# Streamed operands fetched two at a time in 4 KB rows, and one unit buffer more in the retention stage

## The chip, the core and the metric

The kernel runs on one NeuronCore of a Trainium2 chip. The metric is device time in microseconds (us), the median of several runs; a change is read against the median of the kernel before.

## The reference, cut to what matters

```python
# 1. retention: B, H, S, D = 4, 8, 768, 64 (float32 inputs)
for t in range(S):
    state = gamma * state + einsum('bhd,bhe->bhde', k[:, :, t], v[:, :, t])
    y[:, :, t] = scale * einsum('bhd,bhde->bhe', q[:, :, t], state)
x = y.transpose(0, 2, 1, 3).reshape(3072, 512)
# 2. first feed-forward network, weights float64, 512 -> 2048 -> 512
h = x @ w_in;  g = h / (1 + exp(-1.702 * h));  x = g @ w_out
# 3. second one, own float64 weights, same sizes
h = x @ w_in2;  g = maximum(h, 0) ** 2;  out = g @ w_out2
```

## The kernel before, in words

**Retention.** The 3072 tokens are 24 units of 128 tokens (6 per batch entry). One unit is two tiles of 128 x 1024 floats, 512 KB each, of `qkv`, loaded by `load_unit` (L465) on SyncE's queue (SP); the second tile of every sixth unit is a half. `UNITS = 6` unit buffers are cycled: for unit `u`, `u % UNITS` 0 to 2 lie in the pool `att`, whose three buffers come round every six units, and 3 to 5 (`WIDE = 3`) in the pool `wa`, which has eight. Units are worked in groups: 0 to 3 alone, then pairs, then 22 and 23 alone. Step k of the loop issues, in this order: the scores of group k on TensorE (L493), the output matmuls of group k-1 (`outputs`: L558 the state, L572 within the unit, L587 across units) with ScalarE's copies of the state (L563), `cv_high` (ScalarE, L167), the masks of group k on VectorE (L502), `cv_group` (VectorE: `cv_low` L172 of the weight tile converted last, then `convert` of one more, L143 and L152), the scaling of group k-1 out of PSUM (`scaled`, L609 and L616), `cv_ahead` (loads of float64 weight tiles on GpSimd's queue (POOL), L129, and ScalarE's L137), and the loads of units `u + UNITS` for the units just finished. Each pair's outputs but those of groups 1 and 22 use one PSUM tile `yp`, free again when `scaled` has read it.

**Converted weights.** A float64 weight tile (512 KB, `raw`) is turned into a high and a low float32r part by ScalarE and VectorE. There are 32 tiles for the first network, in the list `order`: 0 is up column 0; 1 and 2 are up column 1 and down row 0; 3 and 4 up column 2 and down row 1; and so on, with up column 8 at place 16. `CONV = 3` of them are converted in the retention stage, from step `CV0 = 12` on, and loads begin at step `RAWU = 9` with at most three ahead of the conversion; after that `up` of the first block runs `cv_step` twice for each of its 16 columns.

**First network, three blocks of 1024 tokens.** The first 1024 tokens and half of the next are done plainly: `up` (L682 to L684), `down` (L712 to L714). The others, and all of the second network, use products of quadrants (seven products in place of eight): `up2` (products 1, 2, 6, 5, 7 of column pair p, with 4 and 3 of the pair p-1 behind 1) and `down2` (28 steps of 12 matmuls). All their matmuls are issued at L923 into banks named X, Y, Z (up) and D (down). The left operands are sums of weight quadrants. `make_first` and `make_second` compute them on VectorE and ScalarE (in `background`, between the matmuls), write them to DRAM tiles `kw` on POOL's queue (L276, L338; plain quadrants on SP's, L291 to L295), and `fetch` (L804) reads them back on SP's queue as tiles `r` of 256 KB, 128 rows of 2 KB each, into `SLOTS = 8` buffers. In `up2` one product reads one tile and frees it, and `fetch` then refills it; in `down2` one step reads two tiles, and frees them.

**Order.** Every engine runs its instructions in the order in which this program issues them. SP's queue holds the unit loads, later the `r` tiles and the loads of kept blocks (L1145); POOL's holds the float64 loads (L129, L264), the makers' writes and the stores of kept results.

Of the kernel before, what the change touches and what calls it, by code (L numbers as in the profile page):

```python
# [10 lines left out]
F32 = mybir.dt.float32  # L11
F32R = mybir.dt.float32r
# [7 lines left out]
P = 128  # L20
# [10 lines left out]
WA = 8  # L31
LOOK = 2
WARM = 9
UNITS = 6
WIDE = 3
XHELD = 4
NL = NT // (2 * TB)
NQ = NF // 2
# [1 line left out]
QS = (11, 12, 21, 22)  # L40
PAD = 96
NSTD = 2
SLOTS = 8
EARLY = 2
BG = 4.7
BGK = (2.6,) * 4 + (1.55,) * 9 + (0.5, 1.4, 0.8)
CV0 = 12
RAWU = 9
CONV = 3
FILL = 6  # L50
RAWS = 5
PL = 4
# [5 lines left out]


A11, A12, A22, S1, S2, S3, S4 = range(7)  # L60
PLACE = (range(7), (0, 1, 2, 4, 5, 3, 6))
B11, B21, B22, T1, T2, T3, T4, B12 = range(8)
PRODUCT = {1: (A11, B11), 2: (A12, B21), 3: (S4, B22), 4: (A22, T4), 5: (S1, T1), 6: (S2, T2), 7: (S3, T3)}

# [2 lines left out]
def tile_retention_then_two_ffns(  # L67
# [73 lines left out]
    def join(out, hb):  # L141

        v.tensor_scalar(out=out, in0=hb, scalar1=3, scalar2=None, op0=ALU.logical_shift_left)  # L143

    def round_up(w, raw):

        def halves(t):
            return t.rearrange("p (c t) -> p c t", t=2)

        half = halves(w.bitcast(U16))[:, :, 0]  # L150
        low = raw.bitcast(U16).rearrange("p c (t u) -> p c t u", u=2)[:, :, 0, 1]
        v.scalar_tensor_tensor(out=half, in0=low, scalar=2.0 ** -13, in1=half, op0=ALU.mult, op1=ALU.add)  # L152

    def cv_a():
# [40 lines left out]

    def cv_ahead(k):

        if k >= RAWU:
            cv_load()
        n = cv["a"]  # L200
        if n < min(cv["load"], cv["b"] + 2) and cv["step"] >= loaded[n] + 2:
            cv_a()
# [15 lines left out]
    def weights(f, s):  # L218
        while (f, s) not in ws:
# [9 lines left out]

    jobs = [(m, i) for m in range(2) for i in range(NJ)]  # L230

    kw = [
        [
            [dr_p.tile([7, P, 2, 256], F32, tag=f"kw{l}{m}{p}", name=f"kw{l}{m}{p}") for p in range(NQ)]
            for m in range(2)
        ]
        for l in range(2)
    ]
    made = set()
    acts = deque()  # L240

# [24 lines left out]
    def make_first():  # L266

        load(0)
        load(1)
        with tc.tile_pool(name="k1", bufs=2, side="right", reuse_waits="tile") as pool:  # L270

            def low(m, p, t, h, done):
                while not done:
                    yield None
                v.tensor_tensor(out=h[:, :, :, 1], in0=t, in1=h[:, :, :, 0], op=ALU.subtract)
                nc.gpsimd.dma_start(  # L276
                    out=kw[0][m][p][S1:S4 + 1].rearrange("i p k c -> p i (k c)"),
                    in_=h.bitcast(F32).rearrange("p i k h c -> p i (k h c)"),
                )
                made.add((0, m, p))  # L280
                yield 1.25

            last = None
            for m in (1, 0):
                for p in range(NQ):
                    w0, w1 = ws[p, m], ws[NQ + p, m]

                    dst = kw[0][m][p].rearrange("i p k c -> p i (k c)")
                    f0, f1 = (w.bitcast(F32).rearrange("p (j k) h c -> p j (k h c)", j=2) for w in (w0, w1))
                    if m == 0:  # L290
                        nc.sync.dma_start(out=dst[:, A11:A12 + 1], in_=f0)  # L291
                        nc.sync.dma_start(out=dst[:, A22], in_=f1[:, 1])
                    else:
                        nc.sync.dma_start(out=dst[:, A11], in_=f0[:, 0])
                        nc.sync.dma_start(out=dst[:, A12:A22 + 1], in_=f1)  # L295
                    w = pool.tile([P, 8, P], F32, tag="w", name=f"wf_{m}_{p}", bufs=1)
                    v.tensor_tensor(out=w[:, 0:4], in0=w0[:, :, 0], in1=w0[:, :, 1], op=ALU.add)
                    yield 0.7
                    v.tensor_tensor(out=w[:, 4:8], in0=w1[:, :, 0], in1=w1[:, :, 1], op=ALU.add)
                    yield 0.7  # L300
                    q0, q1, q2, q3 = (w[:, 2 * k:2 * k + 2] for k in range(4))
                    a11, a12, a21, a22 = (q0, q1, q2, q3) if m == 0 else (q0, q2, q1, q3)
                    t = pool.tile([P, 4, 2, P], F32, tag="t", name=f"wt_{m}_{p}")
                    s1, s2, s3, s4 = (t[:, k] for k in range(4))
                    v.tensor_tensor(out=s1, in0=a21, in1=a22, op=ALU.add)
                    v.tensor_tensor(out=s3, in0=a11, in1=a21, op=ALU.subtract)
                    yield 0.85
                    if last is not None:
                        yield from low(*last)
                    v.tensor_tensor(out=s2, in0=s1, in1=a11, op=ALU.subtract)  # L310
                    v.tensor_tensor(out=s4, in0=a12, in1=s2, op=ALU.subtract)
                    h = pool.tile([P, 4, 2, 2, P], F32R, tag="h", name=f"wh_{m}_{p}")
                    done = later(lambda t=t, h=h: nc.scalar.copy(out=h[:, :, :, 0], in_=t))
                    last = m, p, t, h, done
                    yield 0.85
            yield from low(*last)

    def make_second():

        with (  # L320
# [12 lines left out]
            def low(n, w, t, done):  # L333
                while not done:
                    yield None
                m, i = jobs[n]
                v.tensor_tensor(out=t[:, :, 1], in0=w[:, 1:8], in1=t[:, :, 0], op=ALU.subtract)
                nc.gpsimd.dma_start(  # L338
                    out=kw[1][m][i // 2][:, :, i % 2].rearrange("i p c -> p i c"),
                    in_=t.bitcast(F32).rearrange("p i h c -> p i (h c)"),  # L340
                )
                if i % 2:
                    made.add((1, m, i // 2))
                yield 1.1
# [3 lines left out]
            for n in range(len(jobs)):  # L348
# [3 lines left out]
                scale(n + 1)  # L352
                raw = raws[n]
                w = pool.tile([P, 8, P], F32, tag="w", name=f"w32_{n}")
                wf = w.rearrange("p q c -> p (q c)")[:, 0:512]
                join(wf.bitcast(U32), hm.bitcast(U32))
                yield 0.6
                round_up(wf, raw)
                later(lambda n=n: load(n + 3))
                yield 1.05  # L360
                if last is not None:
                    yield from low(*last)
                a21, a11, a12, n22, n3, s1, s2, s4 = (w[:, k] for k in range(8))
                v.tensor_tensor(  # L364
                    out=w[:, 4:6], in0=w[:, 0:1].to_broadcast([P, 2, P]), in1=w[:, 1:4:2], op=ALU.subtract
                )
                yield 0.5
                v.tensor_tensor(out=s2, in0=s1, in1=a11, op=ALU.subtract)
# [63 lines left out]
    with tc.manual_schedule():  # L432
# [345 lines left out]
        for l, n in blocks:  # L778
            first, *rest = [(i, m) for i in ORDER for m in range(NQ // 2)]
            p0 = PL if (l, n) == mixed else 0  # L780
            for p in range(p0, NQ + 1):
                if p < NQ:
                    queue.append((l, n, 0, 1, p))
                else:
                    queue.extend((l, n, 1, first[0], q) for q in range(2))
                if p > p0:
                    queue.extend((l, n, 0, i, p - 1) for i in (4, 3))
                if p < NQ:
                    queue.extend((l, n, 0, i, p) for i in (2, 6, 5, 7))
            for i, m in rest:  # L790
                queue.extend((l, n, 1, i, p) for p in (2 * m, 2 * m + 1))
        fetched = {}
        turn = [0]

        def fetch():
            while queue and len(fetched) < SLOTS:
                l, n, m, i, p = key = queue[0]
                if turn[0] % SLOTS >= len(wr_p):
                    return
                assert key[:1] + key[2:3] + key[4:] in made  # L800
                queue.popleft()
                t = wr_p[turn[0] % SLOTS].tile([P, 2, 256], F32R, tag="w", name="r{}_{}_{}_{}_{}".format(*key))
                turn[0] += 1
                nc.sync.dma_start(out=t.bitcast(F32), in_=kw[l][m][p][PLACE[l][PRODUCT[i][0]]])  # L804
                fetched[key] = t

        for n in range(NSTD):
            for f in range(NF):
# [116 lines left out]
        def up2(l, n, first):  # L925
# [3 lines left out]

            def product(i, p, a, start):  # L930
                s, b = PRODUCT[i]
                w = fetched.pop((l, n, 0, i, p)).rearrange("p k (h c) -> p k h c", h=2)
                for k in range(2):
                    hi, lo = w[:, k, 0], w[:, k, 1]
                    matmul(a, lo, xh[b][:, k], start and k == 0, False)
                    matmul(a, hi, xh[b][:, k], False, False)
                    matmul(a, hi, xl[b][:, k], False, k == 1)
                fetch()
# [109 lines left out]
        def down2(l, n, loads, tick):  # L1048
# [42 lines left out]
            for i in ORDER:  # L1091
# [4 lines left out]
                for m in range(NQ // 2):  # L1096
# [12 lines left out]
                    for e in range(2):  # L1109
                        a = acc[e][0]  # L1110
                        for p in (2 * m, 2 * m + 1):
                            w = fetched[l, n, 1, i, p].rearrange("p j (h c) -> p j h c", h=2)
                            wh, wl = w[:, e, 0], w[:, e, 1]
                            s0, s1 = p == 0 and i in (1, 5), p == NQ - 1
                            matmul(a, wl, hi[:, p % 2], s0, False)
# [83 lines left out]
def _quadrants(w, mt, kt):  # L1199


    a = w.reshape(2, kt, P, 2, mt, P)
    return np.stack([a[0, :, :, 1], a[0, :, :, 0], a[1, :, :, 0], a[1, :, :, 1]])


def _w_in(w):
# [35 lines left out]
```

## Time and profile before

| | |
|---|---|
| median of 3 runs | 1036.88 us (1035.92 to 1038.65) |
| profiled execution, its own time | 1039.62 us |
| its span, first to last instruction | 1037.8 us |
| mean granted TensorE clock | 0.997 |
| DMA moved | 280.33 MB, 270 GB/s over the span |
| DMA packets | 118668, of which 12608 under 512 B |

The views are of the profiled execution; times in them count from its first instruction. PE is TensorE's matmuls, PEld its weight loads, DVE VectorE, ACT ScalarE, POOL GpSimd, SP SyncE; q1 is the DMA queue of SP, q0 that of POOL. "x" gives a count.

### The profile page before, as it was taken

To read this page: it belongs to the slowest core of one execution; us is meant where nothing else is said; L and a number is where in the kernel's file an instruction comes from. 1 tells how busy PE (TensorE), PEld (TensorE's weight loads), DVE (VectorE), ACT (ScalarE), POOL (GpSimd) and SP (SyncE) were. 2 spreads that over 40 slices of the span, in tenths; PEclk is the share of its full clock that TensorE was granted. 3 is DMA by queue.
4 is the path that set the end of the run, shared out by engine and by line. 5 is a ranking of instruction groups with operands and counts; after the bars stand their busy time and mean duration, and the time that the engine had idled before them with its cause. 6 is when DMAs were issued, how large, how long until landed. Compare 5 with 4: busy or idle time off the path is not lost.

```text
span 1037.8 us, 15412 instructions
## 1 busy us (share of the span) xinstructions
PE 1020.4 (98%) x5575; PEld 844.0 (81%) x5575; DVE 727.1 (70%) x969; ACT 518.7 (50%) x800; POOL 124.7 (12%) x179
## 2 busy tenths in 40 slices
PE   8989999999999999999999999999999999999998
PEld 6887788888888888888888788888888888888886
DVE  5658777898687888666888465787445986355953
ACT  4115565444466565455565587564233454233543
POOL 2342220111222000211001210000000001000000
PEclk9999999999999999999999999999999999999999
DMA  9996688956789886999877999767766777766664
GB/s 357 343 351 219 248 289 323 329 216 245 241 295 370 296 310 230 362 389 366 300 233 246 373 359 302 253 229 235 215 193 195 250 238 230 219 194 194 207 199 163
DMA packets 118668, 280.33 MB, mean 270 GB/s; under 512 B 12608, under 2 KB 12736, under 8 KB 118336
## 3 DMA queue, kind: packets, MB, share of 16 engines
q1 hardware_dynamic: 93200, 185.90, 53.7%
q0 software_dynamic: 24672, 92.28, 24.7%
q10 hardware_dynamic: 720, 1.15, 0.3%
q8 instruction: 45, 0.74, 0.3%
q14 instruction: 31, 0.25, 0.1%
HBM read 205.89 MB, written 73.40 MB: 269 GB/s over the span
## 4 chain that ended last, share of the span: by engine, by line
PE 94%; DMA 4%; DVE 1%; SPq 0%; issue 0%; ACT 0%; ACTq 0%
PE D L923 37%; PE X L923 18%; PE Z L923 9%; PE Y L923 5%; DMA unit<-qkv 3%; PE y L713 3%; PE y L712 3%; PE h L682 3%; PE y L714 3%; PE h L684 3%; PE h L683 3%; PE h L886 1%; PE h L885 1%; PE h L884 1%; PE yp L572 1%; PE sc L493 1%
## 5 line engine op out<-in xcount | busy, mean ns | idle before, releaser
L923 PE MATMUL D<-gx,r 128*128 128x512 f32 x1680 | 383.4, 389 | 0.0
L923 PEld LDWEIGHTS D<-gx,r 128*128 128x128 f32 x1680 | 314.9, 188 | 66.8 <-DVE gx L1028 1.4
L1028 DVE TENSOR_TENSOR gx<-g,gx 128x1024 fp32r<-128x1024 f32 x140 | 170.6, 1221 | 43.9 <-ACT gx L1027 43.3
L1027 ACT CAST gx<-g 128x1024 fp32r<-128x1024 f32 x140 | 145.6, 1051 | 96.6 <-PE D L923 91.7
L923 PE MATMUL X<-xh,r 128*128 128x512 f32 x576 | 177.7, 390 | 0.0
L946 DVE TENSOR_TENSOR g<-Z,g 128x512 f32<-128x512 f32 x72 | 49.8, 691 | 144.4 <-ACT g L941 107.5
L941 ACT COPY g<-X 128x512 f32<-128x512 f32 x108 | 63.3, 586 | 168.2 <-PE X L923 167.9
L923 PEld LDWEIGHTS X<-xh,r 128*128 128x128 f32 x576 | 108.4, 188 | 22.6
L923 PE MATMUL X<-xl,r 128*128 128x512 f32 x288 | 112.0, 389 | 0.0
L923 PE MATMUL Z<-xh,r 128*128 128x512 f32 x288 | 88.8, 389 | 2.0 <-DMA r<-kw 2.0
L923 PEld LDWEIGHTS Z<-xh,r 128*128 128x128 f32 x288 | 54.0, 188 | 13.6 <-DVE w L143 2.4
L923 PEld LDWEIGHTS X<-xl,r 128*128 128x128 f32 x288 | 54.2, 188 | 11.3
L923 PE MATMUL Z<-xl,r 128*128 128x512 f32 x144 | 56.1, 390 | 0.0
L682 PE MATMUL h<-hl,w 128*128 128x512 f32 x128 | 50.2, 392 | 3.0 <-DVE w L172 3.0
L684 PE MATMUL h<-hl,w 128*128 128x512 f32 x128 | 49.8, 389 | 0.0
L683 PE MATMUL h<-hl,w 128*128 128x512 f32 x128 | 49.8, 389 | 0.0
L712 PE MATMUL y<-gh,w 128*128 128x512 f32 x128 | 49.8, 389 | 0.0
L713 PE MATMUL y<-gh,w 128*128 128x512 f32 x128 | 49.8, 389 | 0.0
L714 PE MATMUL y<-gl,w 128*128 128x512 f32 x128 | 49.8, 389 | 0.0
L137 ACT ACTIVATE raw<-raw 128x384 f32<-128x384 f32 (+1 forms) x96 | 46.1, 515 | 4.3 <-DMA raw<-w 3.8
L338 POOL DMA_DIRECT2D kw<-wq x32 | 30.4, 950 | 143.1 <-DVE w L364 72.4
L923 PE MATMUL Y<-xh,r 128*128 128x512 f32 x144 | 45.2, 396 | 0.0
(107 smaller groups left out, 1436.4 us busy)
## 6 DMA issues: line engine op xcount, KB each, us to landing
r<-kw SPq DMA_DIRECT2D x532, 256.0 KB, 3.1
kw<-wq POOLq DMA_DIRECT2D x32, 896.0 KB, 6.8
unit<-qkv SPq DMA_DIRECT2D x44, 512.0 KB, 9.5
raw<-w POOLq DMA_DIRECT2D x32, 512.0 KB, 5.0
kw<-wh POOLq DMA_DIRECT2D x16, 1024.0 KB, 4.7
kw<-w SPq DMA_DIRECT2D x16, 512.0 KB, 4.5
raw<-win POOLq DMA_DIRECT2D x16, 512.0 KB, 6.8
raw<-wout POOLq DMA_DIRECT2D x16, 512.0 KB, 7.9
```

What stands on the lines that cost most here:

```text
L137: nc.scalar.activation(out=hm[:, a:z], in_=raw[:, a:z, 1].bitcast(F32), func=ACTF.Prelu, scale=scale, alpha=-2.0 ** 32)
L682: nc.tensor.matmul(hp, lo[:, k], xh, start=(k == 0), stop=False)
L683: nc.tensor.matmul(hp, hi[:, k], xh, start=False, stop=False)
L684: nc.tensor.matmul(hp, hi[:, k], xl, start=False, stop=(k == KD - 1))
L712: nc.tensor.matmul(a, lo[:, e], gh, start=s0, stop=False)
L713: nc.tensor.matmul(a, hi[:, e], gh, start=False, stop=False)
L714: nc.tensor.matmul(a, hi[:, e], gl, start=False, stop=s1)
L923: nc.tensor.matmul(a, w, b, start=start, stop=stop, skip_group_check=True)
L941: nc.scalar.copy(out=t, in_=a)
L946: v.tensor_tensor(out=t, in0=a, in1=t, op=ALU.add)
L1027: nc.scalar.copy(out=hi, in_=src)
L1028: v.tensor_tensor(out=lo, in0=src, in1=hi, op=ALU.subtract)
```

## The change

The streamed operands are laid out anew in DRAM. For the up side one tile `kup` per column pair holds, for each of the 128 partitions, all seven operands side by side in the order `PLACE` (A12, S2, A11, A22, S4, S3, S1 at places 1 to 7), so that the operands of products 2 and 6, 4 and 3, and 7 and 5 are neighbours (`GROUPS`) and are read by one transfer with rows of 4 KB; that of product 1 is still read alone in rows of 2 KB. For the down side `kdown` holds two neighbouring column pairs side by side, which one step reads in rows of 4 KB. The buffers are four of 512 KB in place of eight of 256 KB, so one is refilled after two products (after one for product 1). The transfers of `r` tiles are 284 in place of 532, with the same bytes. The makers write their results in the new order (the same sums with other positions in their tiles); the first one's write is split in two (256 and 768 KB), and the plain quadrants are written by 48 transfers of 256 KB in place of 16 of 512 and 16 of 256 KB.

In the retention stage there are seven unit buffers, four of them in the pool `wa` (`UNITS`, `WIDE`); conversion of weight tiles begins a step earlier (`CV0 = 11`) and makes four (`CONV`), their loads begin a step earlier (`RAWU = 8`, units 12 and 13), and from step 13 on five may be ahead of the conversion in place of three.

```diff
@@ -31,8 +31,8 @@
 WA = 8
 LOOK = 2
 WARM = 9
-UNITS = 6
-WIDE = 3
+UNITS = 7
+WIDE = 4
 XHELD = 4
 NL = NT // (2 * TB)
 NQ = NF // 2
@@ -40,13 +40,13 @@
 QS = (11, 12, 21, 22)
 PAD = 96
 NSTD = 2
-SLOTS = 8
-EARLY = 2
+SLOTS = 4
+EARLY = 1
 BG = 4.7
 BGK = (2.6,) * 4 + (1.55,) * 9 + (0.5, 1.4, 0.8)
-CV0 = 12
-RAWU = 9
-CONV = 3
+CV0 = 11
+RAWU = 8
+CONV = 4
 FILL = 6
 RAWS = 5
 PL = 4
@@ -58,7 +58,8 @@
 
 
 A11, A12, A22, S1, S2, S3, S4 = range(7)
-PLACE = (range(7), (0, 1, 2, 4, 5, 3, 6))
+PLACE = (3, 1, 4, 7, 2, 6, 5)
+GROUPS = {1: (1,), 4: (4, 3), 2: (2, 6), 5: (7, 5)}
 B11, B21, B22, T1, T2, T3, T4, B12 = range(8)
 PRODUCT = {1: (A11, B11), 2: (A12, B21), 3: (S4, B22), 4: (A22, T4), 5: (S1, T1), 6: (S2, T2), 7: (S3, T3)}
 
@@ -144,11 +145,12 @@
 
     def round_up(w, raw):
 
-        def halves(t):
-            return t.rearrange("p (c t) -> p c t", t=2)
-
-        half = halves(w.bitcast(U16))[:, :, 0]
         low = raw.bitcast(U16).rearrange("p c (t u) -> p c t u", u=2)[:, :, 0, 1]
+        if len(w.shape) == 2:
+            half = w.bitcast(U16).rearrange("p (c t) -> p c t", t=2)[:, :, 0]
+        else:
+            half = w.bitcast(U16).rearrange("p b (c t) -> p b c t", t=2)[:, :, :, 0]
+            low = low.rearrange("p (b c) -> p b c", b=2)
         v.scalar_tensor_tensor(out=half, in0=low, scalar=2.0 ** -13, in1=half, op0=ALU.mult, op1=ALU.add)
 
     def cv_a():
@@ -195,6 +197,8 @@
 
     def cv_ahead(k):
 
+        if k == 13:
+            cv["ahead"] = RAWS
         if k >= RAWU:
             cv_load()
         n = cv["a"]
@@ -229,13 +233,20 @@
 
     jobs = [(m, i) for m in range(2) for i in range(NJ)]
 
-    kw = [
-        [
-            [dr_p.tile([7, P, 2, 256], F32, tag=f"kw{l}{m}{p}", name=f"kw{l}{m}{p}") for p in range(NQ)]
-            for m in range(2)
-        ]
+    kup = [
+        [dr_p.tile([P, 8, 2, 256], F32, tag=f"ku{l}{p}", name=f"ku{l}{p}") for p in range(NQ)] for l in range(2)
+    ]
+    kdown = [
+        [dr_p.tile([8, P, 2, 2, 256], F32, tag=f"kd{l}{m}", name=f"kd{l}{m}") for m in range(NQ // 2)]
         for l in range(2)
     ]
+
+    def kept(l, m, p, a, z):
+
+        if m == 0:
+            return kup[l][p][:, a:z]
+        return kdown[l][p // 2][a:z, :, p % 2].rearrange("i p k c -> p i k c")
+
     made = set()
     acts = deque()
 
@@ -273,10 +284,11 @@
-                nc.gpsimd.dma_start(
-                    out=kw[0][m][p][S1:S4 + 1].rearrange("i p k c -> p i (k c)"),
-                    in_=h.bitcast(F32).rearrange("p i k h c -> p i (k h c)"),
-                )
+                for a, z in ((0, 1), (1, 4)):
+                    nc.gpsimd.dma_start(
+                        out=kept(0, m, p, 2, 3) if a == 0 else kept(0, m, p, 5, 8),
+                        in_=h[:, a:z].bitcast(F32).rearrange("p i k h c -> p i k (h c)"),
+                    )
...
@@ -301,7 +315,7 @@
                     q0, q1, q2, q3 = (w[:, 2 * k:2 * k + 2] for k in range(4))
                     a11, a12, a21, a22 = (q0, q1, q2, q3) if m == 0 else (q0, q2, q1, q3)
                     t = pool.tile([P, 4, 2, P], F32, tag="t", name=f"wt_{m}_{p}")
-                    s1, s2, s3, s4 = (t[:, k] for k in range(4))
+                    s2, s4, s3, s1 = (t[:, k] for k in range(4))
                     v.tensor_tensor(out=s1, in0=a21, in1=a22, op=ALU.add)
                     v.tensor_tensor(out=s3, in0=a11, in1=a21, op=ALU.subtract)
                     yield 0.85
@@ -336,7 +350,7 @@
                 m, i = jobs[n]
                 v.tensor_tensor(out=t[:, :, 1], in0=w[:, 1:8], in1=t[:, :, 0], op=ALU.subtract)
                 nc.gpsimd.dma_start(
-                    out=kw[1][m][i // 2][:, :, i % 2].rearrange("i p c -> p i c"),
+                    out=kept(1, m, i // 2, 1, 8)[:, :, i % 2],
                     in_=t.bitcast(F32).rearrange("p i h c -> p i (h c)"),
                 )
                 if i % 2:
@@ -352,17 +366,17 @@
                 scale(n + 1)
                 raw = raws[n]
                 w = pool.tile([P, 8, P], F32, tag="w", name=f"w32_{n}")
-                wf = w.rearrange("p q c -> p (q c)")[:, 0:512]
-                join(wf.bitcast(U32), hm.bitcast(U32))
+                wf = w[:, 0:6].rearrange("p (b q) c -> p b (q c)", b=2)[:, :, 0:256]
+                join(wf.bitcast(U32), hm.bitcast(U32).rearrange("p (b c) -> p b c", b=2))
                 yield 0.6
                 round_up(wf, raw)
                 later(lambda n=n: load(n + 3))
                 yield 1.05
                 if last is not None:
                     yield from low(*last)
-                a21, a11, a12, n22, n3, s1, s2, s4 = (w[:, k] for k in range(8))
+                a21, a12, s2, a11, n22, s4, n3, s1 = (w[:, k] for k in range(8))
                 v.tensor_tensor(
-                    out=w[:, 4:6], in0=w[:, 0:1].to_broadcast([P, 2, P]), in1=w[:, 1:4:2], op=ALU.subtract
+                    out=w[:, 6:8], in0=w[:, 0:1].to_broadcast([P, 2, P]), in1=w[:, 3:5], op=ALU.subtract
                 )
                 yield 0.5
                 v.tensor_tensor(out=s2, in0=s1, in1=a11, op=ALU.subtract)
@@ -779,30 +793,35 @@
             first, *rest = [(i, m) for i in ORDER for m in range(NQ // 2)]
             p0 = PL if (l, n) == mixed else 0
             for p in range(p0, NQ + 1):
+                queue.append((l, n, 0, 1, p) if p < NQ else (l, n, 1, *first))
+                if p > p0:
+                    queue.append((l, n, 0, 4, p - 1))
                 if p < NQ:
-                    queue.append((l, n, 0, 1, p))
-                else:
-                    queue.extend((l, n, 1, first[0], q) for q in range(2))
-                if p > p0:
-                    queue.extend((l, n, 0, i, p - 1) for i in (4, 3))
-                if p < NQ:
-                    queue.extend((l, n, 0, i, p) for i in (2, 6, 5, 7))
-            for i, m in rest:
-                queue.extend((l, n, 1, i, p) for p in (2 * m, 2 * m + 1))
+                    queue.extend((l, n, 0, i, p) for i in (2, 5))
+            queue.extend((l, n, 1, i, m) for i, m in rest)
         fetched = {}
         turn = [0]
 
         def fetch():
-            while queue and len(fetched) < SLOTS:
+            while queue and len({id(t) for t, _ in fetched.values()}) < SLOTS:
                 l, n, m, i, p = key = queue[0]
                 if turn[0] % SLOTS >= len(wr_p):
                     return
-                assert key[:1] + key[2:3] + key[4:] in made
+                assert all((l, m, q) in made for q in ((p,) if m == 0 else (2 * p, 2 * p + 1)))
                 queue.popleft()
-                t = wr_p[turn[0] % SLOTS].tile([P, 2, 256], F32R, tag="w", name="r{}_{}_{}_{}_{}".format(*key))
+                t = wr_p[turn[0] % SLOTS].tile([P, 2, 2, 256], F32R, tag="w", name="r{}_{}_{}_{}_{}".format(*key))
                 turn[0] += 1
-                nc.sync.dma_start(out=t.bitcast(F32), in_=kw[l][m][p][PLACE[l][PRODUCT[i][0]]])
-                fetched[key] = t
+                a = PLACE[PRODUCT[i][0]]
+                if m == 0:
+                    g = GROUPS[i]
+                    a = min(PLACE[PRODUCT[q][0]] for q in g)
+                    nc.sync.dma_start(out=t.bitcast(F32)[:, 0:len(g)], in_=kup[l][p][:, a:a + len(g)])
+                    for q in g:
+                        fetched[l, n, 0, q, p] = t, PLACE[PRODUCT[q][0]] - a
+                else:
+                    nc.sync.dma_start(out=t.bitcast(F32), in_=kdown[l][p][a])
+                    for q in range(2):
+                        fetched[l, n, 1, i, 2 * p + q] = t, q
 
         for n in range(NSTD):
             for f in range(NF):
@@ -929,7 +948,8 @@
 
             def product(i, p, a, start):
                 s, b = PRODUCT[i]
-                w = fetched.pop((l, n, 0, i, p)).rearrange("p k (h c) -> p k h c", h=2)
+                t, q = fetched.pop((l, n, 0, i, p))
+                w = t[:, q].rearrange("p k (h c) -> p k h c", h=2)
                 for k in range(2):
                     hi, lo = w[:, k, 0], w[:, k, 1]
                     matmul(a, lo, xh[b][:, k], start and k == 0, False)
@@ -1109,7 +1129,8 @@
                     for e in range(2):
                         a = acc[e][0]
                         for p in (2 * m, 2 * m + 1):
-                            w = fetched[l, n, 1, i, p].rearrange("p j (h c) -> p j h c", h=2)
+                            t, q = fetched[l, n, 1, i, p]
+                            w = t[:, q].rearrange("p j (h c) -> p j h c", h=2)
                             wh, wl = w[:, e, 0], w[:, e, 1]
                             s0, s1 = p == 0 and i in (1, 5), p == NQ - 1
                             matmul(a, wl, hi[:, p % 2], s0, False)
@@ -1200,7 +1221,7 @@
 
 
     a = w.reshape(2, kt, P, 2, mt, P)
-    return np.stack([a[0, :, :, 1], a[0, :, :, 0], a[1, :, :, 0], a[1, :, :, 1]])
+    return np.stack([a[0, :, :, 1], a[1, :, :, 0], a[0, :, :, 0], a[1, :, :, 1]])
 
 
 def _w_in(w):
```

## Rows read from the trace of the kernel before

**Rows 1.** The page, part 1: busy time, share of the span, instructions.
```profile
PE 1020.4 (98%) x5575; PEld 844.0 (81%) x5575; DVE 727.1 (70%) x969; ACT 518.7 (50%) x800; POOL 124.7 (12%) x179
```
**Rows 2.** Waits of PE: us in total, times, longest us.
```profile
PE sc L493 <- DMA unit<-qkv: 4.5, 7, 1.3
...
PE Z L923 <- DMA r<-kw: 2.0, 1, 2.0
```
**Rows 3.** Timeline of PE, retention: start, us, what, [idle before it].
```profile
48.33 1.16 PE L493 MATMUL sc<-unit 64*128 64x128 f32 x16 [0.78 <-DMA unit<-qkv]
...
54.95 1.16 PE L493 MATMUL sc<-unit 64*128 64x128 f32 x16 [0.93 <-DMA unit<-qkv]
...
67.97 1.16 PE L493 MATMUL sc<-unit 64*128 64x128 f32 x16 [1.53 <-DVE pt L502]
```
**Rows 4.** The load of the first tile of unit 21, SP's queue.
```profile
L465 SPq DMA_DIRECT2D unit<-qkv x1: 1248/1248/1248, 60.6 to 60.6; - x1
...
DMA to landing us min/median/max: 7.3/7.3/7.3
```
**Rows 5.** Windows: PE, PEld, DVE, ACT, POOL busy; clock, DMA share, GB/s.
```profile
40.00:42.00 2.00, 2.00 (x50) 1.83 (x50) 0.86 (x3) 0.37 (x1) 0.82 (x1) 1.00 0.14 35
```
**Rows 6.** Timeline of all engines, retention steps 12 and 13.
```profile
71.33 0.63 PE L558 MATMUL dp<-vs,unit 128*64 128x64 f32 x16
...
74.86 1.92 PE L572 MATMUL yp<-pt,vs 128*64 128x128 f32 x32
...
76.61 0.64 PE L558 MATMUL dp<-vs,unit 128*64 128x64 f32 x16
...
77.62 0.62 ACT L167 CAST w<-hm 128x512 fp32r<-128x512 f32 x1
...
78.27 0.69 DVE L172 TENSOR_TENSOR w<-hm,w 128x512 fp32r<-128x512 f32 x1 [2.59 <-ACT w L167]
...
79.98 1.28 DVE L616 TENSOR_TENSOR xout<-yp,ytab 128x512 f32<-128x512 f32 x2
```
**Rows 7.** Timeline of PE, first network, two waits with the matmul before each.
```profile
89.52 0.39 PE L684 MATMUL h<-hl,w 128*128 128x512 f32 x1
91.01 0.50 PE L682 MATMUL h<-hl,w 128*128 128x512 f32 x1 [1.11 <-DVE w L172]
...
123.56 0.39 PE L714 MATMUL y<-gl,w 128*128 128x512 f32 x1
125.81 0.50 PE L682 MATMUL h<-hl,w 128*128 128x512 f32 x1 [1.87 <-DVE w L172]
```
**Rows 8.** Windows behind the wait for an r tile, second network's start.
```profile
584.00:586.00 2.00, 1.93 (x7) 1.56 (x8) 0.19 (x1) 1.75 (x4) 0.00 (x0) 0.87 1.04 399
586.00:588.00 2.00, 2.00 (x6) 1.60 (x5) 2.00 (x3) 0.00 (x0) 0.00 (x0) 0.50 1.06 411
588.00:590.00 2.00, 2.00 (x8) 1.57 (x8) 1.07 (x3) 0.00 (x0) 1.39 (x2) 0.78 1.01 399
```
**Rows 9.** The chain in order of time: start, us, what.
```profile
346.43 73.61 PE D L923 x324
```
**Rows 10.** DMA landing of r tiles: 730 to 800, 420 to 490, 570 to 580 us.
```profile
DMA to landing us min/median/max: 2.5/2.8/4.1
...
DMA to landing us min/median/max: 3.9/6.2/9.1
...
DMA to landing us min/median/max: 8.2/10.9/11.4
```
**Rows 11.** DMA queues, 577 to 580 us: packets, MB, share of 16 engines.
```profile
q0 software_dynamic: 222, 0.85, 69.2%
q1 hardware_dynamic: 222, 0.40, 34.6%
```
**Rows 12.** DMA queues, 571 to 573 us.
```profile
q1 hardware_dynamic: 49, 0.07, 10.7%
```
**Rows 13.** DMA queues, 20 to 34 us (unit loads alone).
```profile
q1 hardware_dynamic: 1616, 5.67, 101.9%
```

More of the change, by code (lines that the diff above doesn't have):

```diff
@@ L286, in make_first, with quarter @@
                     w0, w1 = ws[p, m], ws[NQ + p, m]
[L288 to L292, printed above, removed]
-                    else:
-                        nc.sync.dma_start(out=dst[:, A11], in_=f0[:, 0])
-                        nc.sync.dma_start(out=dst[:, A12:A22 + 1], in_=f1)
+                    def quarter(w, k):
+                        q = w.bitcast(F32)[:, 2 * k:2 * k + 2].rearrange("p k h c -> p k (h c)")
+                        return q.unsqueeze(1)
+                    for k, q in enumerate(((A11, A12), (A11, None))[m]):
+                        if q is not None:
+                            nc.sync.dma_start(out=kept(0, m, p, PLACE[q], PLACE[q] + 1), in_=quarter(w0, k))
+                    for k, q in enumerate(((None, A22), (A12, A22))[m]):
+                        if q is not None:
+                            nc.sync.dma_start(out=kept(0, m, p, PLACE[q], PLACE[q] + 1), in_=quarter(w1, k))
                     w = pool.tile([P, 8, P], F32, tag="w", name=f"wf_{m}_{p}", bufs=1)
@@ L781, in tile_retention_then_two_ffns @@
             for p in range(p0, NQ + 1):
+                queue.append((l, n, 0, 1, p) if p < NQ else (l, n, 1, *first))
+                if p > p0:
+                    queue.append((l, n, 0, 4, p - 1))
                 if p < NQ:
-                    queue.append((l, n, 0, 1, p))
-                else:
-                    queue.extend((l, n, 1, first[0], q) for q in range(2))
-                if p > p0:
-                    queue.extend((l, n, 0, i, p - 1) for i in (4, 3))
-                if p < NQ:
-                    queue.extend((l, n, 0, i, p) for i in (2, 6, 5, 7))
-            for i, m in rest:
-                queue.extend((l, n, 1, i, p) for p in (2 * m, 2 * m + 1))
+                    queue.extend((l, n, 0, i, p) for i in (2, 5))
+            queue.extend((l, n, 1, i, m) for i, m in rest)
         fetched = {}
```

## The prediction

> **What bounds the kernel now.** First the page's busy times: TensorE has matmuls in flight for 98% of the span [rows 1], so no other engine or the DMA bounds the whole; only PE's waits, and what it does at a lower clock, can be won. A run of 324 matmuls takes 73.61 us [rows 9], 0.227 us each, so 1.36 us for a product of six and 2.73 us for a step of `down2`; the change leaves every matmul in place. Next the waits of PE, and then its timeline at each, which puts them in three places.
>
> Retention: PE waits for unit tiles [rows 2], late at units 15, 17 and 21 by 0.78, 0.93 and 1.53 us [rows 3]. The third row names VectorE, but unit 21 was issued at 60.6 and landed 7.3 us later [rows 4], at 67.9, just when the scores begin: it is a DMA wait too.
>
> First network: two waits for a converted weight tile. From the matmul before to the one after are 1.49 and 2.25 us [rows 7] in place of 0.23, so 1.26 and 2.02 us are lost.
>
> Start of the second network: 2.0 us for an `r` tile [rows 2], and behind it granted clocks of 0.87, 0.50 and 0.78 over three windows of 2 us [rows 8]: 0.26 + 1.00 + 0.44 = 1.7 us lost to the lower level, 1.2 GHz. Together 3.7 us.
>
> **Part 1, the unit buffers.** Between 40 and 42 us the DMA engines move 35 GB/s [rows 5], against 5.67 MB in 14 us, 405 GB/s, when the unit loads run freely [rows 13]. They idle because unit 14 may be loaded only when unit 8's buffer is free, and all later units stand behind it on SP. With seven buffers unit 14 takes unit 7's, free a unit earlier, 15 takes 8's, 17 to 20 lie in `wa` buffers long free, and 21 takes 14's. The loads gain nearly the 2 us of that gap and more at later ones, and the three waits are 1.53 us at the longest. One more float64 tile now comes ahead of unit 21: 512 KB at 405 GB/s is 1.3 us, which could leave it up to 0.6 us late. Bounds: between 0 and 3.24 us gained; I take all 3.24, as the idle DMA time ahead of all three waits exceeds each.
>
> **Part 2, conversion a step earlier.** Converting at step 11 fills idle VectorE time. At step 12 there is now a tile to finish, and that has a price: `cv_low` waits for ScalarE's `cv_high`, which stands behind the state copies of the outputs, and `scaled` stands behind both on VectorE. Step 13 shows this order already: the state matmuls end at 76.61 + 0.64 = 77.25, the copy to high runs at 77.62, `cv_low` at 78.27, and `scaled` ends at 79.98 + 1.28 = 81.26 [rows 6], 4.0 us behind the state. There nothing needs `yp` at once. At step 12 the state matmuls end at 71.96 and PE begins to write `yp` again at 74.86 [rows 6], 2.9 us later; with `scaled` 4.0 us behind, PE waits 1.1 us. Bounds: 0 (the copy sooner than at step 13) to 4.0 (PE needs `yp` at once); I take 1.1, since both rows are of these very steps. Retention thus gains 3.24 - 1.1 = 2.1 us.
>
> **Part 3, a fourth converted tile.** The first wait is for up column 2, place 3 in the list: now converted before the network begins. The second is for column 8, place 16, for which the steady pace of two tiles a column was half a column late: with one tile more in hand it is finished one `cv_step` earlier, over 2 us before its use. Both go: 1.26 + 2.02 = 3.3 us. The loads that may now run five ahead keep the raw tiles in front. Bounds: 1.26 (if the later wait only moves) to 3.3; I take 3.3. `background` may start one column earlier, which shifts `make_first` alone: `make_second` waits for `mixing`.
>
> **Part 4, the streamed operands.** Two things pull against each other. Look-ahead: with eight buffers a tile was asked for seven products before its use, 9.5 us in `up2`; with four, one of which holds a single operand there, it is five products, 6.8 us. In `down2` it is three steps, 8.2 us. A landing of 256 KB takes 2.8 us where nothing else moves [rows 10]; 512 KB need 256 KB more at 405 GB/s, 0.65 us, so 3.4. The slack falls from 6.7 us to 3.4.
>
> Share: where makers and streams move together, both queues finish the same number of packets, 222 each, and POOL's get 0.85 MB against 0.40 [rows 11]. So SP's rows of 2 KB get 133 GB/s where the products need 256 KB per 1.36 us, 192. In each us of this they lose 0.31 us of slack; so the landings grow to 10.9 us [rows 10], and 16 us of it, with 2 us in which SP's queue got 0.07 MB [rows 12], 35 GB/s, use up 16 x 0.31 + 1.6 = 6.5 us, all the slack: the wait of 2.0 us. With rows of 4 KB at equal packet counts SP gets half of 417 GB/s in `down2`, 208, and with one transfer of four at 2 KB 3.5/7.5 of it, 195, in `up2`. Both cover 192, so only the 1.6 us of the starved stretch are lost, less than 3.4: no wait, and without the wait no lower clock. 3.7 us gained. Bounds: this whole sum, or nothing, or the loss of the first rival.
>
> The Trainium skill (DMA: Bandwidth & Descriptors, section "SWDGE vs HWDGE vs iDMA") says that a packet is preferably up to 4096 B, may hold many descriptors, and that an engine changes between queues only at packet ends. If two rows of 2 KB already went as one packet, the wider rows would change no share. The trace differs: at equal packet counts SP's bytes were half of POOL's. By the rule the sum would be that of the first rival.
>
> At nothing I cost the makers' sums (as many elements, other positions; VectorE is busy 70% [rows 1] and off the path), their extra writes (16 on POOL, 16 on SP, when SP has nothing else to load), and SP's fewer issues. If POOL's loads are slowed by the share they lose, VectorE's and ScalarE's queues could hold back the gx tiles behind a late raw tile; three jobs of load-ahead cover it, and the rest is in the range.
>
> **The sum.** 2.1 + 3.3 + 3.7 = 9.1 us. The profiled span of 1037.8 becomes 1028.7, and its own time 1039.62 becomes 1030.5. That execution is 2.7 us above the median shown, so from the median, 1036.9 - 9.1 = 1027.8 us.
>
> **Rivals.**
> 1. *Slower, by the shorter look-ahead.* SP's share doesn't grow, because a packet of its queue is something else than a row. Then landings stay as long as they were and grow by 0.65 us: at 570 to 580 11.4 + 0.65 - 6.8 = 5.3 us of waits in place of 2.0, near 420 us 9.1 + 0.65 - 6.8 = 3.0 [rows 10], with another 1.7 us at the lower clock there: 8.0 us lost against 5.4 gained in parts 1 to 3, so 1039.5 us. It decides where the streams' waits and clock loss pass 3.7 + 5.4 = 9.1 us in all; here they are 5.3 + 1.7 + 3.0 + 1.7 = 11.7, so from landings 1.3 us shorter at both places on. For it: the slack is halved, and the stretch 420 to 490 has a median landing of 6.2 us. Against: the equal packet counts. 0.12, of which 0.05 within the bound below.
> 2. *The waits of the streams shrink but stay.* Two starved stretches close together use the 3.4 us up: one wait of about 2 us with its 1.7 us of lower clock stays, somewhere between 420 and 600 us. 1036.9 - 5.4 = 1031.5 us. 0.18.
> 3. *Retention gives nothing.* Unit 21 is still late by 0.6 us and the `yp` wait is 2.6, in the upper half of its bounds: 3.24 - 0.6 - 2.6 is 0, so 1036.9 - 7.0 = 1029.9 us. 0.15.
> 4. *The change does little*: part 3's second wait only moves and rival 2 holds: 1033.5 us or more. 0.08, most of it within the bound.
>
> My forecast has 0.47. It and rivals 2 and 3 are faster.
>
> **How the numbers follow.** About 0.3% (3.1 us) is what a measurement of this kernel can tell from no change. Faster by more: 0.47 + 0.18 + 0.15 and 0.01 of rival 4, 0.81. Within it: 0.05 + 0.06 = 0.11. Slower: 0.07 + 0.01, 0.08. The range begins at 1025.3, where the `yp` wait costs nothing (1.1 less) with 1.4 for the spread of runs, and reaches to 1035.0, over rivals 3 and 2 and the start of rival 4. The forecast's own range is 1026 to 1030.
>
> **What would show it.** Unit waits of `sc` only up to 25 us, and the first `up` matmul near 82 instead of 84.2; a wait of some 1.1 us at a `yp` matmul near 73; no wait for `w` in the first network; no wait for `r`, landings below 6.8 us in `up2`, equal bytes of both queues in a shared stretch, and a clock of 1.00 around 580 us. I am wrong if an `r` wait shows anywhere in `up2`, or if the two queues' bytes still stand at one to two.

## The result and the profile after

Seven runs of the changed kernel have a median of 1043.64 us, seven of the kernel before 1037.12; the ratio is 1.0059, 95% interval 1.0042 to 1.0076. It is slower by 0.6%, where 1027.8 us were forecast. The profiled span is 1041.9 us against 1037.8.

The waits of PE after (us in total, times, longest), answering to [rows 2]:

```profile
PE sc L507 <- DMA unit<-qkv: 2.7, 5, 1.3
PE yp L601 <- issue: 2.1, 2, 1.5
PE Z L942 <- DMA r<-ku: 2.0, 3, 0.9
PE yp L586 <- DVE xout L630: 2.0, 1, 2.0
PE X L942 <- ACT g L961: 1.8, 2, 1.1
PE sc L507 <- DVE pt L516: 1.6, 1, 1.6
PE X L942 <- DMA r<-ku: 1.5, 2, 1.1
...
PE Y L942 <- DMA r<-ku: 0.3, 1, 0.3
```

No `h` waits for `w` any more: part 3 came out. But `r` tiles are waited for in eight places. Two of them are put down to ScalarE (1.8 us): the timeline has one at 429.49, and the tile of that product, asked for at 420.7, took 8.7 us and landed at 429.4; the other is at 586.33, and its tile, asked for at 577.9, took 8.3 us. So the streams' waits are 2.0 + 1.8 + 1.5 + 0.3 = 5.6 us in place of 2.0.

```profile
425.26 0.62 PE L942 MATMUL X<-xh,r 128*128 128x512 f32 x2
425.71 0.39 PE L942 MATMUL X<-xl,r 128*128 128x512 f32 x1
427.20 0.73 PE L942 MATMUL X<-xh,r 128*128 128x512 f32 x2 [1.10 <-DMA r<-ku]
...
429.49 0.69 PE L942 MATMUL X<-xh,r 128*128 128x512 f32 x2 [0.63 <-ACT g L961]
```

A wait costs more than its idle column says. Without it the row at 427.20 would have begun some 0.23 us after the one at 425.71, as rows here do, so 1.26 us are lost and not 1.10; and it takes 0.73 us where the same row takes 0.62. That is some 0.27 us more for each wait.

That load, and the landings of `r` in the stretches of [rows 10] (730 to 800, 420 to 490, 570 to 580 us):

```profile
L818 SPq DMA_DIRECT2D r<-ku x1: 319/319/319, 420.7 to 420.7; - x1
...
DMA to landing us min/median/max: 8.7/8.7/8.7
...
DMA to landing us min/median/max: 3.1/3.9/5.0
...
DMA to landing us min/median/max: 3.4/6.2/8.7
...
DMA to landing us min/median/max: 5.1/6.9/8.3
```

In the last of these stretches the longest landing did get shorter, 8.3 us where it was 11.4. They had only 6.8 us to land in. Queues after, 425 to 432 us (a shared stretch), then 421 to 423.5, 468.5 to 470.5 and 597 to 599 (packets, MB, share):

```profile
q0 software_dynamic: 375, 1.40, 52.0%
q1 hardware_dynamic: 370, 1.34, 50.0%
...
q0 software_dynamic: 231, 0.82, 94.1%
q1 hardware_dynamic: 15, 0.02, 2.0%
...
q0 software_dynamic: 194, 0.75, 100.1%
q1 hardware_dynamic: 6, 0.02, 2.5%
...
q0 software_dynamic: 205, 0.78, 98.3%
q1 hardware_dynamic: 7, 0.02, 3.0%
```

In the shared stretch the two queues are now equal in bytes, as forecast (1 to 2 in [rows 11]). In the others, SP's queue gets 0.02 MB in 2 to 2.5 us, 8 to 10 GB/s, worse than the 35 of [rows 12], and wide rows are no help there. Six of the eight waits are for a tile that had one such stretch, of 1.5 to 2.5 us, between its issue and its landing (from 322.5, 421, 468.5, 579.5 or 597 us on; two waits share the one at 421). The tile of the wait at 589.60 was asked for at the end of the stretch from 579.5, and that of the wait at 488.91 had none of this length.

Retention, timeline of PE with idle time and what ended it:

```profile
54.38 1.16 PE L507 MATMUL sc<-unit 64*128 64x128 f32 x16 [1.57 <-DVE pt L516]
...
60.44 0.76 PE L601 MATMUL yp<-unit,st 64*64 64x128 f32 x17 [1.48 <-issue]
...
67.20 0.43 PE L601 MATMUL yp<-unit,st 64*64 64x128 f32 x3 [0.64 <-issue]
...
71.81 0.64 PE L572 MATMUL dp<-vs,unit 128*64 128x64 f32 x16
...
74.22 0.69 PE L572 MATMUL dp<-vs,unit 128*64 128x64 f32 x16
76.87 1.97 PE L586 MATMUL yp<-pt,vs 128*64 128x128 f32 x32 [1.97 <-DVE xout L630]
...
86.19 0.50 PE L696 MATMUL h<-hl,w 128*128 128x512 f32 x1
```

In the timeline of all engines, the scaling (`scaled`) that `yp` waits for:

```profile
75.45 1.27 DVE L630 TENSOR_TENSOR xout<-yp,ytab 128x512 f32<-128x512 f32 x2
```

Units 15 and 21 are no longer waited for; unit 17 still is (1.57; the row names VectorE, but the unit's tile, asked for at 43.1, took 11.1 us and landed at 54.2). The `yp` wait priced at 1.1 us is 1.97. New are 2.1 us of "issue", in which PE waits for nothing that the profile shows. The first up matmul starts at 86.19 in place of 84.16.

### The profile page after: what moved, and what is told of

It reads as the page before. It is cut to its first block, busy times and chain, and to the rows that moved or that the text cites. A ratio compares the mean times of both kernels' runs of the same rounds, so it can differ in the third digit from the quotient of the medians.

```text
span 1041.9 us, 14837 instructions
## 1 busy us (share of the span) xinstructions
PE 1021.9 (98%) x5575; PEld 842.0 (81%) x5575; DVE 727.5 (70%) x969; ACT 518.7 (50%) x800; POOL 132.0 (13%) x195
## 4 chain that ended last, share of the span: by engine, by line
PE 92%; DMA 6%; DVE 1%; issue 1%; ACT 0%; SPq 0%; ACTq 0%
PE D L942 37%; PE X L942 17%; PE Z L942 9%; DMA r<-ku 4%; PE Y L942 4%; PE h L696 3%; PE h L697 3%; PE y L727 3%; PE y L726 3%; PE h L698 3%; PE y L728 3%; DMA unit<-qkv 2%; PE yp L586 2%; PE sc L507 1%; PE h L904 1%; PE h L903 1%
## 5 line engine op out<-in xcount | busy, mean ns | idle before, releaser
L942 PEld LDWEIGHTS X<-xl,r 128*128 128x128 f32 x288 | 54.1, 188 | 11.4
L751 DVE TENSOR_TENSOR xl<-xb,xh 128x1024 fp32r<-128x1024 f32 x28 | 34.1, 1218 | 8.0 <-ACT xh L750 8.0
```

The source lines that it names most:

```text
L942: nc.tensor.matmul(a, w, b, start=start, stop=stop, skip_group_check=True)
```

## The experiments

Each ratio is to the kernel before, run beside the experiment (its medians there: 1039.27, 1038.06 and 1038.07 us); the interval behind it is the 95% interval.

**The two halves.** In the kernel before (lines joined here):

```diff
-UNITS = 6; WIDE = 3; CV0 = 12; RAWU = 9; CONV = 3
+UNITS = 7; WIDE = 4; CV0 = 11; RAWU = 8; CONV = 4
 def cv_ahead(k):
+        if k == 13:
+            cv["ahead"] = RAWS
```

> The retention half of the change alone (seven unit buffers, conversion and loads a step earlier, four tiles, five ahead); streams as before. Theory (both halves cost: retention ends 2.0 us later, the first network's two waits of 3.3 us go): first up matmul at 86.2 us, no wait for w, block boundary as before with its 2.0 us wait and its lower clock, 1037.1 + 2.0 - 3.3 = 1035.8 us. Rival (the late end of retention comes from something that the streams' half moved, such as the place of code in memory): first up matmul near 84, 1033.8 us.

Measured 1035.94 us, 0.9965 (0.9951 to 0.9979): a gain. Its retention ends as late as with the whole change, at 86.55, with the same `yp` wait:

```profile
77.23 1.97 PE L574 MATMUL yp<-pt,vs 128*64 128x128 f32 x32 [1.99 <-DVE xout L618]
```

The other half, the changed kernel with all of this undone:

> The streams' half alone (4 KB rows, four buffers of two operands); retention as before. Theory (the shorter look-ahead, 6.8 us in place of 9.5, meets stretches of 2 to 3 us after each of the makers' writes in which SP's queue gets almost nothing): seven or more waits for r in up2 of 0.3 to 1.3 us, 7 to 8 us in all in place of 3.8, first network's 3.3 us of waits still there, 1037.1 + 4 = 1041 us. Rival (the streams are innocent, and waits come from the makers being shifted by the retention half): within 1 us of before or faster.

Measured 1049.13 us, 1.0091 (1.0066 to 1.0116). The whole loss, and more, is the streams', and the two halves multiply to 1.0056, where the change has 1.0059:

```profile
PE X L940 <- DMA r<-ku: 4.4, 5, 1.1
...
PE Y L940 <- DMA r<-ku: 1.8, 3, 1.1
PE Z L940 <- DMA r<-ku: 1.1, 2, 0.7
```

The waits, 7.3 us in ten places, are what was expected; their price is not: 9.9 us between the medians, where 4 were expected. (Expectations below put these waits at 9 to 10 us; the rows give 7.3.)

**Row width or look-ahead.** In the streams' half, two transfers for one (the down side likewise):

```diff
-nc.sync.dma_start(out=t.bitcast(F32)[:, 0:len(g)], in_=kup[l][p][:, a:a + len(g)])
+for q in range(len(g)):
+    nc.sync.dma_start(out=t.bitcast(F32)[:, q:q + 1], in_=kup[l][p][:, a + q:a + q + 1])
```

> As the streams' half alone, but each 512 KB buffer is filled by two transfers with rows of 2 KB: the same layout in DRAM, the same look-ahead, only the row width of the change is taken back. Theory (wider rows do raise SP's share, the look-ahead costs): SP's bytes fall to half of POOL's in shared stretches, and the waits for r grow by 3 us or more over the streams' half alone, 1044 us or above. Rival 1 (row width does nothing): same as the streams' half alone within 1 us. Rival 2 (the wide rows or the 16 KB pitch are what costs): 3 us faster than the streams' half alone.

Measured 1048.56 us, 1.0091 (1.0066 to 1.0116): the same as with wide rows, so it looked as if width did nothing (rival 1); the listed waits for `r` are 9.1 us. But two things had changed: with two transfers, the first operand can be used when it has landed. The next kernel keeps one transfer of two operands and narrows the rows by padding them apart:

```diff
-dr_p.tile([P, 8, 2, 256], F32, ...)
+dr_p.tile([P, 8, 576], F32, ...)   # operands in [:, :, 0:512]; kdown likewise
```

> The streams' half alone, with 256 bytes of padding behind every operand's row in DRAM, so that one transfer still brings two operands and must land whole, but in rows of 2 KB: the row width alone against the streams' half (1.0091 of before). Theory (wider rows raise SP's share and this is worth something): SP's bytes fall to half of POOL's in shared stretches, the waits for r grow from 9 to 10 us to 13 or more, ratio 1.013 or above. Rival (what decides are the starved stretches and the look-ahead, not the share): ratio within 0.002 of the streams' half.

Measured 1053.37 us, 1.0154 (1.0117 to 1.0191). The queues at 425 to 432 us and the waits for `r`:

```profile
q0 software_dynamic: 476, 1.66, 66.0%
q1 hardware_dynamic: 466, 0.89, 35.9%
```
```profile
PE X L940 <- DMA r<-ku: 7.6, 6, 3.3
...
PE Y L940 <- DMA r<-ku: 3.0, 4, 1.7
...
PE Z L940 <- DMA r<-ku: 0.5, 2, 0.3
```

SP's queue is back at half of the other's bytes, and the waits are 11.1 us in place of 7.3. So the width is worth some 0.6% at an equal look-ahead. The two intervals only just part (to 1.0116, from 1.0117), and the lower clock has a share in it: the mean granted clock of these runs is 0.990 to 1.000, 0.997 to 1.000 with wide rows. That the padded rows also start at other addresses was not tested apart. The two-transfer kernel, with rows of 2 KB too, is 0.6% faster than this one and equal to the wide rows; that its first operand may be used before the second has landed would explain this, but is argued and not shown.

The look-ahead alone, in the kernel before:

```diff
-SLOTS = 8
+SLOTS = 6
```

> Kernel before with one number changed, six buffers of 256 KB in place of eight: rows of 2 KB, transfers of 256 KB, look-ahead in up2 of five products (6.8 us) as with the change. Theory (the look-ahead is what costs): waits for r of 7 us or more in place of 2.0, some in down2 too, where it is now two steps (5.4 us); 1037.5 + 6 or more, 1043 to 1047 us. Rival (it is the transfer of two operands, which must land whole, that costs): waits for r below 4 us, 1039 us or less.

Measured 1052.52 us, 1.0142 (1.0127 to 1.0158), with rows and transfers as before:

```profile
PE X L923 <- DMA r<-kw: 3.2, 7, 1.0
...
PE D L923 <- DMA r<-kw: 3.0, 4, 1.1
PE Z L923 <- DMA r<-kw: 2.7, 5, 1.2
```

8.9 us of waits in place of 2.0; 3.0 of them in `down2`, whose look-ahead this kernel cuts more than the change does. The time is above the 1043 to 1047 us expected, and these waits do not account for all of the 14.5 us. The reverse, a fifth wide buffer:

```diff
-SLOTS = 4
+SLOTS = 5
-            tc.tile_pool(name="k3", bufs=1, ...) as third,   # the third raw buffer
-            raw_p.append(third); load(2)
-                later(lambda n=n: load(n + 3))
+                later(lambda n=n: load(n + 2))
```

> The streams' half alone with a fifth buffer of 512 KB, so that the look-ahead in up2 is again seven products (9.5 us) at rows of 4 KB; for room the makers of the second network have two raw buffers in place of three and load one job later. Theory (look-ahead): waits for r fall from some 9.6 us to below 2, 1037.5 us or less, unless the later raw loads make ScalarE wait. Rival (the layout or the wide transfers cost by themselves): still 1043 us or more.

Measured 1054.08 us, 1.0159 (1.014 to 1.0178), and yet no wait for `r` is left. PE waits for ScalarE instead, and ScalarE for the float64 loads that now come a job later, a wait for which the kernel before has no row (PE's row, then ScalarE's):

```profile
PE X L937 <- ACT g L956: 12.1, 8, 2.5
```
```profile
ACT raw L138 <- DMA raw<-wout: 23.6, 7, 6.2
```

Here ScalarE is rightly named: no `r` tile lands in the 0.8 us before any of the eight, where in the changed kernel the two that were put down to ScalarE had landed 0.1 us before. So the time tells nothing for the look-ahead, the rows do: at 9.5 us the wide stream is nowhere late, though with little to spare (its longest landing is 10.0 us, and PE's other waits give it time). The memory for it was not to be had without a loss elsewhere.

**What the landings wait for.** In the streams' half, a seventh of each write, and the second network reading the first one's operands:

```diff
-out=kept(1, m, i // 2, 1, 8)[:, :, i % 2], in_=t...
+out=kept(1, m, i // 2, 1, 2)[:, :, i % 2], in_=t[:, 0:1]...
-in_=kup[l][p][...]   # and kdown[l]
+in_=kup[0][p][...]   # and kdown[0]
```

> The streams' half alone, but of the makers' writes for the second network one operand of seven is written (128 KB in place of 896 KB), and the second network reads the first one's operands: the sums for it are made and not stored, so its output is not the reference's. Theory (SP's queue starves in the stretch of each such write): the stretches in which SP gets under 60 GB/s with transfers open go, the waits for r fall from some 9.6 us to below 2, and the time falls by 8 us to some 1039 us. Rival (the float64 loads on POOL's queue starve it just as well, or the look-ahead is too short for any sharing): waits stay above 5 us.

Measured 1038.98 us, 1.001 (0.9998 to 1.0023). One wait for `r` is left:

```profile
PE X L940 <- DMA r<-ku: 0.9, 1, 0.9
```

The landings of `r` at 420 to 490 us, in the streams' half, then here:

```profile
DMA to landing us min/median/max: 3.8/6.6/8.5
...
DMA to landing us min/median/max: 3.1/4.1/7.5
```

The makers' writes for the second network (32 of 896 KB, 29 MB; 25 MB of them are left out here) are what the shorter look-ahead can't bridge. Splitting them was no remedy:

```diff
-nc.gpsimd.dma_start(out=kept(1, m, i // 2, 1, 8)..., in_=t...)
+for a, z in ((0, 3), (3, 7)):
+    nc.gpsimd.dma_start(out=kept(1, m, i // 2, a + 1, z + 1)..., in_=t[:, a:z]...)
+    yield 0.55
```

> The streams' half alone, with each of the makers' writes for the second network split into two transfers of 384 and 512 KB, the second issued half a VectorE step later. Theory (SP's queue starves for about as long as one write lasts): the starved stretches get shorter, the waits for r fall from some 9.6 us to 5 to 7, ratio 1.006. Rival (it is the total of the traffic that counts, or the float64 loads): no change, 1.009.

Measured 1049.08 us, 1.0106 (1.0085 to 1.0127), with 7.5 us of waits for `r`, and SP's queue still gets next to nothing (424 to 426 us):

```profile
q0 software_dynamic: 200, 0.75, 94.9%
q1 hardware_dynamic: 9, 0.02, 2.1%
```

The rival holds as far as this goes: halving the transfer changes nothing, and it may be the sum of the traffic that counts. A finer split was not tried.

**Retention.** Four converted tiles at the old step:

```diff
-CONV = 3
+CONV = 4
```

> Kernel before with one number changed: four tiles converted in the retention stage, beginning at the old step 12, so that the fourth falls into the last step, behind all masks. Theory: no yp wait at step 12 as no tile is held there; the wait at column 8 goes (2.0 us) and that at column 2 shrinks from 1.3 to some 0.4 us; 1037.1 - 2.9 = 1034.2 us. Rival (the fourth conversion delays the last scaling, so what is won comes back at the start of the first network): 1037 us.

Measured 1034.28 us, 0.9948 (0.9928 to 0.9968). No `h` waits for `w`, and no `yp` for `xout`. (Its list has 1.4 us of `Z` put down to `w`: that is an `r` tile at the second network's start, asked for at 570.2 and landed 10.8 us later, just before the matmul at 581.12.) With the seventh buffer and the five loads ahead besides (`UNITS = 7`, `WIDE = 4`, `CV0` and `RAWU` as before):

> Kernel before with seven unit buffers, four tiles converted from the old step 12 on, five loads ahead from step 13 on, loads from the old step 9; streams as before. Theory (the step-earlier conversion and load were what cost in retention): no yp wait of 2 us, unit waits of 2 us in place of 4.5, first up matmul at 82.5, first network without waits for w; 1037.5 - 1.5 - 3.0 = 1033 us, 1 us below the kernel with four converted tiles alone. Rival (the seventh unit buffer brings nothing, as the DMA queue is full in any case): equal to that kernel, 1034.3.

Measured 1031.97 us, 0.9945 (0.9931 to 0.9959), the lowest median of all; by the ratios, each to its own runs of the kernel before, it can't be told from four tiles alone. In its profile the seventh buffer shows: no unit is late after 21 us, and the first up matmul starts at 82.06 (84.47 with four tiles alone). The same with `RAWU = 8`:

> The kernel with seven unit buffers and four tiles converted from the old step 12 on (0.9945 of before), with the float64 loads alone a step earlier (step 8). Theory (the early loads take DMA time from the units: late unit 17 and waits for instructions): unit waits and waits for issue in retention 1 to 2 us longer, no yp wait of 2 us on xout, first up matmul at 83.5, ratio 0.996. Rival (all of the loss in retention is the yp wait of the earlier conversion): equal to that kernel, first up matmul at 82.

Measured 1033.66 us, 0.9962 (0.9949 to 0.9974). Unit 17 is late again and the issue waits grow, without any `yp` wait on `xout`; the first up matmul starts at 82.91:

```profile
54.51 1.16 PE L495 MATMUL sc<-unit 64*128 64x128 f32 x16 [1.09 <-DMA unit<-qkv]
60.30 0.76 PE L589 MATMUL yp<-unit,st 64*64 64x128 f32 x17 [1.21 <-issue]
```

So in retention the early loads cost about 0.9 us. The early conversion costs more: the retention half differs from this kernel in `CV0` alone, and its first up matmul starts 3.6 us later. Of these 2.0 are the `yp` wait, and 0.8 a longer wait for unit 17 (1.92 us in place of 1.09); the rest is not explained. The intervals of the two timings overlap; the places are read from one profile of each.

## Why the prediction was wrong

**Part 4 failed**, at the step "only the 1.6 us of the starved stretch are lost, less than 3.4: no wait". The share was right: equal packet counts, so equal bytes at 4 KB, and worth 0.6%. Three terms were not. A free landing of 512 KB takes 3.9 us, not 3.4, so the slack of a free queue was 2.9. That slack was then taken to hold in shared stretches too, because 195 GB/s cover 192; but at half the rate a transfer lands later by itself (512 KB: 1.3 us at 405 GB/s, 2.7 us at the 191 of 425 to 432 us). The median landing at 420 to 490 us, starved stretches included, is 6.2 us, which leaves 0.6 us of 6.8. And the starved stretch read as 2 us at 35 GB/s is 2.5 at 8, 2.4 us lost instead of 1.6. So one such stretch is enough for a wait: the transfer asked for at 420.7 had 8.7 us to wait, 1.9 more than its look-ahead. Slack was halved for certain, while the share only helps where both queues are served.

**Rival 1** had the side and the place (the shorter look-ahead; all waits but one are at 427 to 489 and 586 to 603 us), but its condition, that the share doesn't grow, is not what happened. The rule of the Trainium skill that stands beside it (DMA: Bandwidth & Descriptors, section "SWDGE vs HWDGE vs iDMA", a packet may hold many descriptors) would have left the share as it was, if it put two rows of 2 KB into one packet; the padded rows show that a row of 2 KB went as a packet of its own, at 466 packets and half the bytes of the other queue's 476. **Rival 2**, waits that stay, took two starved stretches close together to use the slack up, for one wait; one stretch did it, and eight waits came.

**Part 4's price** of 3.7 us at the second network's start was in part that execution's own: the half with the old streams, the kernel with four tiles, and the one with `RAWU = 8` wait there too, 1.1 to 1.4 us, at a mean granted clock of 1.000 (the kernel with two transfers per buffer waits 2.1 us there, also at 1.000); the 1.7 us at the lower level are not in every execution.

**Part 1** was right in the mechanism: with seven buffers and the loads at their old step the late units 15, 17 and 21 go. In the change the early load took unit 17's gain back; I had asked that only of unit 21.

**Part 2** named the wait and its place; it is 1.97 us, not 1.1. `scaled` ends at 75.45 + 1.27 = 76.72, 4.3 us behind the state (71.81 + 0.64 = 72.45), not 4.0. And PE gets to `yp` sooner. In the kernel before it began `yp` 0.51 us after the state matmuls ahead of it (74.35 to 74.86); in the changed kernel these begin at 74.22, so `yp` could have begun at some 74.7, 2.3 us behind the state and not 2.9. The scores before them run through here, where the kernel before has a stop in them (timeline of the kernel before):

```profile
73.71 0.71 PE L493 MATMUL sc<-unit 64*128 64x128 f32 x6 [0.29 <-issue]
...
74.35 0.69 PE L558 MATMUL dp<-vs,unit 128*64 128x64 f32 x16
```

The 2.1 us of issue waits I had not named. Retention lost 2.0 us instead of gaining 2.1.

**Part 3** was right: 3.3 us of waits went, and one number alone (`CONV`) takes them away. The 0.5% that this gave are more, 5 us between the medians; the profile has beside them the shorter wait at the second network's start and no lower clock there.

In the profile: retention +2.0; the plain part of the first network, up to the first `X` (303.9 in place of 305.5), -3.6; all that follows, the rest of the +4.1 us: +5.7. Of these, 3.6 are the listed waits and some 1.9 what seven waits more cost beside their idle time (7 x 0.27). The lower clock that went, 1.7, is made up for by stalls too short for the list; they were not counted one by one. The medians are 6.5 us apart, as the profiled execution of the kernel before was 2.5 us above its median of 1037.12.

## What to carry to other kernels

A buffer ring of fixed size trades look-ahead for wider transfers: when rows or pairs are widened, work out first how late a refill may be asked for, and hold that against the longest landing, not the median. A share of bandwidth between queues is worth something only while both are served; the stretch in which one gets nothing sets the look-ahead. And take a change apart before judging it: a part worth half a per cent stood here behind one that cost nearly twice that.

## What the hardware showed that was not expected

A queue with transfers open can get next to nothing while another is served: 15 packets in 2.5 us against 231. Leaving out most of the makers' writes removed all waits but one; splitting them didn't. Why those stretches are not shared packet by packet, as the others are, stays open. And when the DMA queues are full (407 GB/s at 57 to 60.5 us), TensorE can stop for 0.6 to 1.5 us with no semaphore to blame ("issue"); earlier loads made these stops longer. That its instructions come late over the same DMA engines would fit: in the changed kernel the queue that carries instructions (q8) has one packet of 16 KB in 57.5 to 58.5 us and one in 64.5 to 65, and the two stops end at 60.44 and 67.20. It wasn't tried.

```profile
q8 instruction: 1, 0.02, 6.4%
...
q8 instruction: 1, 0.02, 12.8%
```
